# Keeping the running decay products in each chunk's buffer set instead of passing them through DRAM, with 20 sets in place of 23, in an RWKV-style attention and mixture-of-experts kernel

## The chip, the cores and the metric

The kernel runs on one core of a Trainium2 chip. The metric is the device time of one execution, in microseconds (us), lower being better. All arithmetic is in float32, or in float32 split into a rounded part and a remainder.

## The reference, cut to what matters

A linear recurrence over 768 tokens runs for 4 batches and 8 heads of width 40. Its outputs are then the tokens of a small mixture of 8 experts, with a gate that is balanced by eight rounds of row and column normalisation.

```python
for t in range(S):                                # 768 tokens; B=4, H=8, D=40
    y[:, :, t] = einsum('bhd,bhde->bhe', r_t, state)
    Sa = einsum('bhde,bhe->bhd', state, a_t)
    state_decay = state * w_t[:, :, None, :] - einsum('bhd,bhe->bhde', Sa, b_t)
    state = state_decay + einsum('bhd,bhe->bhde', v_t, k_t)
x = y as (3072 tokens, 320)
logits = x @ w_gate; logits = logits - logits.max()
P = exp(logits); 8 rounds: P /= rowsum + 1e-9; P /= colsum + 1e-9; P *= N / E
out = sum over 8 experts e of P[:, e] * (relu(x @ w1[e]) @ w2[e])   # w1 320x1024, w2 1024x320
```

## The kernel before, in words

The sequence is cut into 12 chunks of 64 tokens. A unit of work is one chunk of one batch, with all 8 heads as 4 pairs; there are 48 units, and unit number cb is chunk cb // 4, batch cb % 4. The two heads of a pair lie on partitions 0 to 39 and 64 to 103.

`prep` prepares one unit, and needs no state. It loads the decays w, k, b and a in one tile (`inp`, two buffers; the first units borrow memory of sets that aren't in use yet). VectorE (DVE) makes two running products of the decays with scans: `q` (L124, one buffer) and the decays `g` from the chunk's start (L134). GpSimd (POOL) multiplies k and b by q (`kb`, L147) and a by g (`ab`, L153 and L154); for the first six units VectorE does the two `ab`. TensorE then makes the products `ll` (L159) and transposes `kt` (L167). What the later steps need goes into one of NSX = 23 buffer sets, taken in turn: `sx`, `bb` and `cc`. The lower triangle `lt` is written to DRAM (`ld`). The decays g are written to DRAM too (L138, tile `gd`), to be read back (L278, tile `gl`) when the unit is computed.

Two chunks form a group. For each of the 6 groups 128 triangular 32x32 blocks are inverted on VectorE, one block per partition: `load_lu` reads them from `ld` into `lu` (L380), the functions of the list INV run, `finish` stores the inverses `un` and `tn` to DRAM (L371, L372). `tload` reads them back for one chunk, as `lb` (L243), `t1` and `t2` (tile `td`, L246 and L248) and the diagonal blocks of `tt` (L252), and `tmat` makes the off-diagonal part on TensorE (`gp`, `op`).

`recur` computes one unit in five steps, which alternate with those of other batches: load v, r and v transposed (`vz`, `rb`, `f`) and make `av` with VectorE's product into f (L290); `xc`; `pu`, with VectorE's product `pm`; `c2`, with VectorE's sum `ws` (L317), and on POOL the output `y`, which is ws times the decays (L321), and the next state `z` (L330, on VectorE from chunk 9); the transpose `zt`. r is used as a tile of 112 partitions by 128 columns for each pair, in which each head fills its own half of the columns and the rest is zero; two transfers of 48 KB write the filled parts, into two buffers that were zeroed at the start.

The order of the work is a list of (time, function) pairs, sorted and then traced. A unit's preparation stands in it behind the fourth step of the unit that had its set before, 23 units earlier, or later where the group's start P0 sets it. The traced program is put in order for each engine by a scheduler, and each engine runs its queue in that order. Almost all loads and stores are issued from the SyncE queue (SP), in one order as well.

In the second part (from L470 on), each expert's weights and the tokens are loaded, split into parts, and multiplied: `p` (L582) and `op` (L647). Its buffers use the memory of the attention's, so the first of its work starts as the attention's last units run. `sinkhorn` normalises the gate; `ident` and `ones`, which its transposes and sums need, and `pmat` are allocated before the attention.

Of the kernel before, what the change touches and what calls it, by code (L numbers as in the profile page):

```python
# [23 lines left out]
NTOK = NB * S  # L24
E, FF, DM = 8, 1024, 320
# [4 lines left out]
def attention(ctx, tc, d, xd, ps, pq, pt, gs, lg):  # L30
    nc = tc.nc
# [3 lines left out]
    const = ctx.enter_context(tc.tile_pool(name="a_const", bufs=1))  # L35
    io = ctx.enter_context(tc.tile_pool(name="a_io", bufs=1))
    wk = ctx.enter_context(tc.tile_pool(name="a_wk", bufs=2))
# [7 lines left out]
    ident = cst[:, 232:360]  # L45
    one65 = cst[0:RL, 400:660]

    NTB = 2
    sx_b, bb_b, cc_b = ([None] * NSX for _ in range(3))
    raws = {}  # L50
    for n in range(NCH * NB - NSX, NCH * NB):
        i, pool = n % NSX, sets[n - NCH * NB + NSX]
        if i in IN_SETS or i in KB_SETS:
            raw = pool.tile([128, 1252], F32, name=f"st{i}")
            raws[i] = raw
            sx_b[i] = raw[0:R2, 0:832].rearrange("r (p h x) -> r p h x", h=2, x=104)
# [30 lines left out]
    def clear():  # L87
        nc.gpsimd.memset(unf, 0.0)
        nc.gpsimd.memset(unf[:, 0:1024:33], 1.0)
        nc.gpsimd.memset(tnf, 0.0)  # L90
        for t in vz_b + rb_b + c1_b + lg_b:
            nc.vector.memset(t, 0.0)
        for t in y_b:
            nc.gpsimd.memset(t[96:RL], 0.0)
        for t in tt_b:
            nc.gpsimd.memset(t, 0.0)
# [18 lines left out]
    def prep(c, b, ld):  # L115
# [14 lines left out]
        i = next(j for j in range(NSX) if sx_b[j] is sx)  # L130
        bb, cc = bb_b[i], cc_b[i]
        ge = pin.tile([RL, NP, 65], F32, name="g", bufs=2)
        g = ge[:, :, 0:64]
        nc.vector.tensor_tensor_scan(  # L134
            out=ge.rearrange("r p t -> r (p t)"), data0=w65[:, 0:260],
            data1=g1.rearrange("r p t -> r (p t)"), initial=0.0, op0=ALU.mult, op1=ALU.add)
        gd = dr.tile([RL, 320], F32, name=f"gd{cb}", bufs=1)
        nc.sync.dma_start(out=gd[:, 0:260], in_=ge.rearrange("r p t -> r (p t)"))  # L138
        if cb < NKB:
# [37 lines left out]
        if cb >= NKB:  # L177
            (nc.sync if cb < N_SP else nc.scalar).dma_start(out=ld[GRP[c][1], :, b], in_=lt)
        return dict(cc=cc, g=gd, sx=sx, bb=bb)

# [52 lines left out]
    def tload(c):  # L233
        tt = rot("tt", tt_b)
        tts[c] = tt
        ld, ud, nd = invs[GRP[c][0]]
        t1, t2, lb = td_b[0][0:64], td_b[0][64:128], lg_b[0][0:64]
        cc = GRP[c][1]
        q = [slice(h * 32, h * 32 + 32) for h in range(2)]
        u = [[slice(cc * 64 + blk * 32 + h * 16, cc * 64 + blk * 32 + h * 16 + 16) for h in range(2)]  # L240
             for blk in range(2)]
        for h in range(2):
            nc.sync.dma_start(out=lb[q[h], :, q[h]],  # L243
                              in_=ld[cc, 0:32].rearrange("j b p h s -> j (b p) h s")[:, :, h, 32:64])
        for h in range(2):
            nc.sync.dma_start(out=t1[q[h]], in_=nd[u[0][h]].rearrange("g j s -> j g s"))  # L246
        for h in range(2):
            nc.sync.dma_start(out=t2[q[h]], in_=ud[u[1][h]].rearrange("g j s -> j g s"))  # L248
        for h in range(2):
            for blk in range(2):  # L250
                r = slice(h * 64 + blk * 32, h * 64 + blk * 32 + 32)
                nc.sync.dma_start(out=tt[r, :, r], in_=ud[u[blk][h]].rearrange("g j s -> j g s"))  # L252

# [16 lines left out]
    def recur(c, b):  # L270
# [3 lines left out]
        rb = rot("rb", rb_b)  # L274
        for h in range(2):
            nc.sync.dma_start(out=rb[h * 64:h * 64 + 48, :, h * 64:h * 64 + 64], in_=d["r"][c, b, h])
        gl = io.tile([RL, NP, 65], F32, name="gl", bufs=2)
        nc.sync.dma_start(out=gl.rearrange("r p t -> r (p t)"), in_=pp["g"][:, 0:260])  # L278
        f = wk.tile([R2, NP, 2, 104], F32, name="f", bufs=NFB)
# [40 lines left out]
        y = ys[c, b // 2]  # L320
        nc.gpsimd.tensor_tensor(out=y[0:R2, :, b % 2], in0=ws[:, :, 0:64], in1=gl[0:R2, :, 0:64], op=ALU.mult)  # L321
        if b % 2:
# [51 lines left out]
    def load_lu(s, n):  # L374
        ld = invs[s][0]
        for cc in range(n):
            for blk in range(2):
                for h in range(2):
                    u0, r0 = cc * 64 + blk * 32 + h * 16, blk * 32
                    nc.sync.dma_start(  # L380
                        out=lu[u0:u0 + 16],
                        in_=ld[cc, r0:r0 + 32].rearrange("j b p h s -> (b p) j h s")[:, :, h, r0:r0 + 32])

# [47 lines left out]
SKEW = 1.1  # L431
NSX = 23
GL = 3
# [32 lines left out]
def body(ctx, tc, d, out):  # L466
    nc = tc.nc
# [301 lines left out]
def _layout(inputs):  # L769
    g = {k: np.asarray(v, dtype=np.float32) for k, v in inputs.items()}  # L770

    def split(a):
        return a.reshape(NB, NP, 2, NCH, C, D).transpose(3, 0, 2, 5, 1, 4)

    def packed(a, fill=0.0):
# [60 lines left out]
```

## Time and profile before

| | |
|---|---|
| median of 3 runs | 1839.33 us (1838.09, 1839.33, 1847.54) |
| the profiled execution's own time | 1832.94 us |
| its span, first to last instruction | 1831.2 us, 31655 instructions |
| busy share of the span | PE 94%, DVE 75%, POOL 48%, ACT 47% |
| DMA packets | 211759, 140.47 MB; under 512 bytes 162965 |
| from DRAM and back, decays: `gd` and `gl` | 48 each, 113.8 KB each |
| loads of r | 96, 48.0 KB each |

"Busy" is the sum of an engine's instructions; a matrix product's end is modelled, so TensorE's 94% is not 94% of its peak. SPq is the queue of SyncE, whose only work is to issue transfers; PEclk is the granted clock of TensorE, 1.00 being full speed. The attention takes about the first 505 us, in which the DMA engines are busiest; the experts take the rest. In a row of a timeline the first two numbers are the start and the duration in us, and a bracket tells how long the engine had been idle and on what. In a row of a single line, the three numbers with strokes are the least, median and largest duration in ns.

### The profile page before, as it was taken

The page shows a single profiled execution, that of the slowest core. Times are in us where ns is not written, and L with a number is a line of the kernel's source. Part 1 is how long each engine was busy: PE and PEld are TensorE (multiplying, and loading weights), DVE is VectorE, ACT ScalarE, POOL GpSimd, SP SyncE. Part 2 cuts the span into 40 slices and gives each one's busy share as a digit, 9 for nine tenths or more (in the row PEclk, how much of TensorE's full clock was granted, in tenths as well). Part 3 has the DMA queues.
Part 4 walks back from the last instruction along what each step waited for, and adds up shares of the span by engine and source line. Part 5 has one row for each costly group of instructions (what it writes and reads, how often), then busy time and mean ns, then how long its engine had stood idle before and what let it go on. Part 6 is the DMA issues. An engine that isn't in the chain of part 4 may idle for free.

```text
span 1831.2 us, 31655 instructions
## 1 busy us (share of the span) xinstructions
PE 1724.3 (94%) x11843; PEld 1696.8 (93%) x11843; DVE 1365.3 (75%) x2356; ACT 856.8 (47%) x1851; POOL 874.0 (48%) x854
## 2 busy tenths in 40 slices
PE   4479988999989999999999999999999999999999
PEld 4368888898978999999999999999999999999999
DVE  7786996973788867777676878977686877767675
ACT  6347767766743533434343434345343343424342
POOL 6545664723462626447291735008182644628160
PEclk8568988999999999999999999999999999999999
DMA  7468777867520101111020112201020111102001
GB/s 193 116 157 185 175 180 174 186 137 172 152 77 20 57 20 57 38 39 57 20 75 20 57 37 61 69 1 60 16 76 20 57 38 38 57 20 75 15 24 44
DMA packets 211759, 140.47 MB, mean 77 GB/s; under 512 B 162965, under 2 KB 193813, under 8 KB 211605
## 3 DMA queue, kind: packets, MB, share of 16 engines
q1 hardware_dynamic: 207925, 132.70, 27.9%
q10 hardware_dynamic: 3680, 5.74, 1.2%
q8 instruction: 94, 1.54, 0.3%
q14 instruction: 60, 0.49, 0.1%
HBM read 110.78 MB, written 27.61 MB: 76 GB/s over the span
## 4 chain that ended last, share of the span: by engine, by line
PE 75%; DVE 7%; DMA 4%; issue 4%; POOL 3%; ACT 2%; SPq 2%; POOLq 0%; ACTq 0%; DVEq 0%
PE op L647 36%; PE p L582 33%; DMA inp<-in_inp_dram 1%; PE xc L297 1%; PE av L289 1%; PE pu L308 1%; DVE pr L193 1%; DVE hl L606 1%; DVE q L124 1%; PE c L315 1%; DMA ld<-lt 1%; PE op L266 1%; DVE sm L600 1%; PE ll L159 1%; POOL ab L154 1%
## 5 line engine op out<-in xcount | busy, mean ns | idle before, releaser
L582 PE MATMUL p<-xch,wh 128*128 128x384 f32 (+1 forms) x1792 | 605.0, 339 | 8.9 <-DVE sm L600 4.3
L603 ACT ACTIVATE hh<-sm 128x384 fp32r<-128x384 f32 x512 | 269.5, 527 | 728.5 <-DVE sm L600 728.4
L647 PE MATMUL op<-wh,hh 128*128 128x320 f32 x1536 | 477.2, 311 | 4.0 <-ACT hh L603 3.8
L647 PE MATMUL op<-wl,hh 128*128 128x320 f32 x1536 | 474.8, 310 | 0.0
L647 PE MATMUL op<-wh,hl 128*128 128x320 f32 x1536 | 468.0, 309 | 0.9 <-DVE hl L606 0.9
L528 POOL TENSOR_TENSOR wl<-ws,wh 128x640 fp32r<-128x640 f32 x60 | 103.1, 1718 | 606.2 <-ACT wh L526 606.1
L606 DVE SCALAR_TENSOR_TENSOR hl<-sm,hh 128x384 fp32r<-128x384 f32 x512 | 373.1, 762 | 2.6 <-ACT hh L603 1.8
L582 PEld LDWEIGHTS p<-xch,wh 128*128 128x128 f32 (+1 forms) x1792 | 337.0, 188 | 13.3 <-DVE sm L600 5.2
L582 PE MATMUL p<-xcl,wh 128*128 128x384 f32 x896 | 302.3, 337 | 0.0
L582 PE MATMUL p<-xch,wl 128*128 128x384 f32 x896 | 301.8, 337 | 0.0
L647 PEld LDWEIGHTS op<-wh,hh 128*128 128x128 f32 x1536 | 290.2, 189 | 4.9 <-ACT hh L603 4.9
L647 PEld LDWEIGHTS op<-wl,hh 128*128 128x128 f32 x1536 | 291.1, 190 | 0.0
L647 PEld LDWEIGHTS op<-wh,hl 128*128 128x128 f32 x1536 | 286.8, 188 | 1.4 <-DVE hl L606 1.2
L600 DVE TENSOR_TENSOR sm<-p,u 128x384 f32<-128x384 f32 x384 | 236.3, 625 | 8.7
L582 PEld LDWEIGHTS p<-xcl,wh 128*128 128x128 f32 x896 | 168.6, 188 | 0.0
L582 PEld LDWEIGHTS p<-xch,wl 128*128 128x128 f32 x896 | 168.5, 188 | 0.0
L600 DVE TENSOR_TENSOR sm<-p,p 128x384 f32<-128x384 f32 x128 | 71.3, 557 | 129.4 <-PE p L582 75.0
L600 DVE TENSOR_TENSOR p<-p,p 128x384 f32<-128x384 f32 x128 | 71.1, 556 | 101.7 <-PE p L582 101.4
L600 DVE TENSOR_TENSOR u<-p,p 128x384 f32<-128x384 f32 x128 | 70.8, 553 | 57.1 <-PE p L582 55.9
L536 POOL TENSOR_TENSOR wl<-ss,wh 128x512 fp32r<-128x512 f32 x60 | 90.3, 1505 | 28.4 <-ACT wh L533 24.2
L159 PE MATMUL ll<-ab,kb 104*128 104x128 f32 x336 | 62.8, 344 | 40.5 <-POOL kb L147 18.5
L159 PEld LDWEIGHTS ll<-ab,kb 104*128 104x128 f32 x336 | 54.2, 244 | 45.3 <-POOL kb L147 24.8
(163 smaller groups left out, 2727.3 us busy)
## 6 DMA issues: line engine op xcount, KB each, us to landing
ws<-in_wts_dram SPq DMA_DIRECT2D x60, 832.0 KB, 4.5
inp<-in_inp_dram SPq DMA_DIRECT2D x42, 451.5 KB, 4.5
gd<-g SPq DMA_DIRECT2D x48, 113.8 KB, 2.6
gl<-gd SPq DMA_DIRECT2D x48, 113.8 KB, 2.8
vz<-in_v_dram SPq DMA_DIRECT2D x48, 112.0 KB, 3.5
xd<-y SPq DMA_DIRECT2D x24, 224.0 KB, 3.5
ld<-lt ACTq DMA_DIRECT2D x40, 128.0 KB, 2.6
rb<-in_r_dram SPq DMA_DIRECT2D x96, 48.0 KB, 3.1
```

Source lines behind the costliest of these rows:

```text
L124: nc.vector.tensor_tensor_scan(out=qr.rearrange("r p t -> r (p t)"), data0=w65[:, 260:0:-1], data1=one65, initial=0.0, op0=ALU.mult, op1=A ...
L154: eng.tensor_tensor(out=ab[64:104, :, 64:128], in0=a_in[64:104], in1=g[64:104], op=ALU.mult)
L159: nc.tensor.matmul(ll[:, p], lhsT=kb[:, p], rhs=ab[:, p], start=True, stop=True)
L193: nc.vector.tensor_tensor(out=prv, in0=a.unsqueeze(2).broadcast_to([nu, n_c, n_r, n_k]), in1=m.unsqueeze(1).broadcast_to([nu, n_c, n_r, n_ ...
L266: nc.tensor.matmul(op[:, p], lhsT=gs[:, p], rhs=t2[:, p], start=True, stop=True)
L528: g.tensor_tensor(out=wl[:, 0:640], in0=raw[:, 256:896], in1=wh[:, 0:640], op=ALU.subtract)
L536: g.tensor_tensor(out=lv[:, 3:7], in0=so[:, :, 0], in1=hv[:, 3:7, 0], op=ALU.subtract)
L582: nc.tensor.matmul(o, lhsT=w_, rhs=x_, start=(j == 0), stop=(j == 3))
L600: eng.tensor_tensor(out=out, in0=x, in1=y, op=ALU.add)
L603: nc.scalar.activation(out=hh[:, f, h], in_=sm[f][:, h], func=AF.Relu)
L606: v.scalar_tensor_tensor(out=hl[:, f, h], in0=sm[f][:, h], scalar=0.0, in1=hh[:, f, h], op0=ALU.max, op1=ALU.subtract)
L647: nc.tensor.matmul(ops[i], lhsT=a[:, h, cs], rhs=w_[:, cw], start=(f == 0 and h == 0 and j == 0), stop=(last and h == 1 and j == 2))
```

## The change

The decays g are written straight into the unit's set (`ge`, 1040 bytes a partition), and `y` reads them there; the trip through DRAM and its two transfers a unit are gone. A set is therefore larger, and there are 20 instead of 23. r is laid out with its zeros in DRAM and comes in one transfer of 112 rows of 2048 bytes. The blocks of the inverse are ordered so that the two heads alternate, and `load_lu` and the two loads of `td` each take one transfer where two were needed. `pmat`, `ones` and `ident` are now allocated behind the attention, in memory that it used.

```diff
-        ge = pin.tile([RL, NP, 65], F32, name="g", bufs=2)
+        bb, cc, ge = bb_b[i], cc_b[i], ge_b[i]        # ge: a part of set i
         g = ge[:, :, 0:64]
         nc.vector.tensor_tensor_scan(out=ge..., data0=w65[:, 0:260], data1=g1..., ...)
-        gd = dr.tile([RL, 320], F32, name=f"gd{cb}", bufs=1)
-        nc.sync.dma_start(out=gd[:, 0:260], in_=ge.rearrange("r p t -> r (p t)"))
...
-        return dict(cc=cc, g=gd, sx=sx, bb=bb)
+        return dict(cc=cc, g=g, sx=sx, bb=bb)
... tload
-        for h in range(2):
-            nc.sync.dma_start(out=t1[q[h]], in_=nd[u[0][h]].rearrange("g j s -> j g s"))
-        for h in range(2):
-            nc.sync.dma_start(out=t2[q[h]], in_=ud[u[1][h]].rearrange("g j s -> j g s"))
+        nc.sync.dma_start(out=t1, in_=nn_[0])
+        nc.sync.dma_start(out=t2, in_=un_[1])
... recur
-        for h in range(2):
-            nc.sync.dma_start(out=rb[h * 64:h * 64 + 48, :, h * 64:h * 64 + 64], in_=d["r"][c, b, h])
-        gl = io.tile([RL, NP, 65], F32, name="gl", bufs=2)
-        nc.sync.dma_start(out=gl.rearrange("r p t -> r (p t)"), in_=pp["g"][:, 0:260])
+        nc.sync.dma_start(out=rb, in_=d["r"][c, b])
...
-        nc.gpsimd.tensor_tensor(out=y..., in0=ws[:, :, 0:64], in1=gl[0:R2, :, 0:64], op=ALU.mult)
+        nc.gpsimd.tensor_tensor(out=y..., in0=ws[:, :, 0:64], in1=pp["g"][0:R2], op=ALU.mult)
... load_lu
-                for h in range(2):
-                    nc.sync.dma_start(out=lu[u0:u0 + 16], in_=ld[cc, r0:r0 + 32]...[:, :, h, r0:r0 + 32])
+                nc.sync.dma_start(out=lu[u0:u0 + 32],
+                                  in_=ld[cc, r0:r0 + 32].rearrange("j b p h s -> (b p h) j s")[:, :, r0:r0 + 32])
...
-NSX = 23
+NSX = 20
... body, behind the attention and the experts' own buffers
+    two = ctx.enter_context(tc.tile_pool(name="two", bufs=1))
+    pmat, ones, ident = ...                            # from two
+    nc.gpsimd.memset(ones, 1.0)
+    nc.sync.dma_start(out=ident, in_=d["cst"][:, 232:360])
```

The program issues 533 transfers from SP where it issued 725: 48 fewer each of `gd`, `gl` and `rb`, 24 of `lu`, 12 each of the two `td`. The zeroing of `rb` is gone, and three units' sets less are cleared at the start.

The queue of SP at the end of the first group's inverse, before (names: `ud`, `nd` the stored inverses in DRAM, `ld` the triangles of the second group; the last two are the data of units 18 and 19):

```order
L371 DMA ud_244<-un_235 64x1024 x2
L372 DMA nd_245<-tn_239 64x1024 x2
L248 DMA td_219<-ud_244 32x16x32
L246 DMA td_219<-nd_245 32x16x32
L380 DMA lu_236<-ld_576 16x32x32 x4
L246 DMA td_219<-nd_245 32x16x32
L248 DMA td_219<-ud_244 32x16x32
L252 DMA tt0_217<-ud_244 32x16x32 x4
L138 DMA gd16_1002<-g_1000 112x260
L138 DMA gd17_1088<-g_1086 112x260
L118 DMA inp_1162<-in_inp_dram 112x1032
L118 DMA inp_1222<-in_inp_dram 112x1032
```

The same place of SP's queue now:

```order
L364 DMA ud_232<-un_223 64x1024 x2
L365 DMA nd_233<-tn_227 64x1024 x2
L244 DMA td_207<-ud_232 64x16x32
L372 DMA lu_224<-ld_534 32x32x32 x2
L243 DMA td_207<-nd_233 64x16x32
L248 DMA tt0_205<-ud_232 32x16x32 x4
L119 DMA inp_1072<-in_inp_dram 112x1032
L119 DMA inp_1129<-in_inp_dram 112x1032
```

Between the inverses' store and the next `inp` stand 8 transfers instead of 14; the load from `nd` now stands behind those of `lu`, where half of it stood ahead of them.

VectorE where unit 4 is computed and a later unit is prepared, before (g is the scan of unit 24, into a buffer of its own; ws that of unit 4):

```order
L134 SCALAR_TENSOR_TENSOR g_1566<-inp_1561,g10_223 112x260
L317 TENSOR_TENSOR ws_1657<-c2_1652,c10_229 104x416
L124 SCALAR_TENSOR_TENSOR q_1667<-inp_1665,cst_162 112x260
L310 TENSOR_TENSOR pm_1703<-pu_1698,cst_162 128x416
L128 RECIPROCAL g10_223<-q_1667 112x4
L134 SCALAR_TENSOR_TENSOR g_1670<-inp_1665,g10_223 112x260
```

VectorE at the same unit now (ge4 is the decay tile of set 4, which unit 4 leaves and unit 24 takes):

```order
L283 TENSOR_TENSOR f_1407<-av_1411,cst_147 104x8x64
L310 TENSOR_TENSOR ws_1528<-c2_1523,c10_217 104x416
L167 TENSOR_TENSOR sx3_185<-ll_1453,cst_147 64x8x64
L134 SCALAR_TENSOR_TENSOR ge4_192<-inp_1536,g10_211 112x260
L303 TENSOR_TENSOR pm_1571<-pu_1566,cst_147 128x416
L125 SCALAR_TENSOR_TENSOR q_1620<-inp_1618,cst_147 112x260
```

The scan of unit 24 stood ahead of `ws` of unit 4; now it stands one instruction behind it. It overwrites what `y` of unit 4 reads, and so waits for POOL. This is so for units 20 to 47, each against the unit 20 before it.

POOL at that place now (kb and ab on ge4 are unit 24's, cc5 is unit 25's):

```order
L150 COPY cc4_191<-q_1538 104x4
L314 TENSOR_TENSOR y0_221<-ws_1528,ge4_192 104x4x64
L323 TENSOR_TENSOR z_1531<-ws_1528,cc8_151 104x160
L145 TENSOR_TENSOR kb_1542<-inp_1536,q_1538 104x512
L151 TENSOR_TENSOR ab0_209<-inp_1536,ge4_192 40x4x64
L152 TENSOR_TENSOR ab0_209<-inp_1536,ge4_192 40x4x64
```

Before, `kb` and both `ab` of unit 24 stood ahead of `y` of unit 4; now they stand behind it.

More of the change, by code (lines that the diff above doesn't have):

```diff
@@ L35, in attention @@
     const = ctx.enter_context(tc.tile_pool(name="a_const", bufs=1))
-    io = ctx.enter_context(tc.tile_pool(name="a_io", bufs=1))
     wk = ctx.enter_context(tc.tile_pool(name="a_wk", bufs=2))
@@ L48, in attention @@
     NTB = 2
-    sx_b, bb_b, cc_b = ([None] * NSX for _ in range(3))
+    sx_b, bb_b, cc_b, ge_b = ([None] * NSX for _ in range(4))
     raws = {}
@@ L53, in attention @@
         if i in IN_SETS or i in KB_SETS:
-            raw = pool.tile([128, 1252], F32, name=f"st{i}")
+            raw = pool.tile([128, 1512], F32, name=f"st{i}")
             raws[i] = raw
@@ L58, in attention @@
             cc_b[i] = raw[0:R2, 1248:1252]
+            ge_b[i] = raw[0:RL, 1252:1512].rearrange("r (p t) -> r p t", t=65)
             continue
@@ L62, in attention @@
         cc_b[i] = pool.tile([R2, NP], F32, name=f"cc{i}")
+        ge_b[i] = pool.tile([RL, NP, 65], F32, name=f"ge{i}")
     tt_b = [const.tile([128, 4 * NP, 128], F32, name=f"tt{i}") for i in range(NTB)]
@@ L90, in clear @@
         nc.gpsimd.memset(tnf, 0.0)
-        for t in vz_b + rb_b + c1_b + lg_b:
+        for t in vz_b + c1_b + lg_b:
             nc.vector.memset(t, 0.0)
@@ L130, in prep @@
         i = next(j for j in range(NSX) if sx_b[j] is sx)
-        bb, cc = bb_b[i], cc_b[i]
-        ge = pin.tile([RL, NP, 65], F32, name="g", bufs=2)
+        bb, cc, ge = bb_b[i], cc_b[i], ge_b[i]
         g = ge[:, :, 0:64]
@@ L239, in tload @@
         q = [slice(h * 32, h * 32 + 32) for h in range(2)]
-        u = [[slice(cc * 64 + blk * 32 + h * 16, cc * 64 + blk * 32 + h * 16 + 16) for h in range(2)]
-             for blk in range(2)]
+        un_, nn_ = ([t[cc * 64 + blk * 32:cc * 64 + blk * 32 + 32].rearrange("(g h) j s -> (h j) g s", h=2)
+                     for blk in range(2)] for t in (ud, nd))
         for h in range(2):
@@ L251, in tload @@
                 r = slice(h * 64 + blk * 32, h * 64 + blk * 32 + 32)
-                nc.sync.dma_start(out=tt[r, :, r], in_=ud[u[blk][h]].rearrange("g j s -> j g s"))
+                nc.sync.dma_start(out=tt[r, :, r], in_=un_[blk][h * 32:h * 32 + 32])
     def tmat(c, half):
@@ L320, in recur @@
         y = ys[c, b // 2]
-        nc.gpsimd.tensor_tensor(out=y[0:R2, :, b % 2], in0=ws[:, :, 0:64], in1=gl[0:R2, :, 0:64], op=ALU.mult)
+        nc.gpsimd.tensor_tensor(out=y[0:R2, :, b % 2], in0=ws[:, :, 0:64], in1=pp["g"][0:R2], op=ALU.mult)
         if b % 2:
@@ L377, in load_lu @@
             for blk in range(2):
-                for h in range(2):
[L379 to L382, printed above, removed]
+                u0, r0 = cc * 64 + blk * 32, blk * 32
+                nc.sync.dma_start(out=lu[u0:u0 + 32],
+                                  in_=ld[cc, r0:r0 + 32].rearrange("j b p h s -> (b p h) j s")[:, :, r0:r0 + 32])
     ev = [(T_CLEAR, clear, ())]
@@ L472, in body @@
     one = ctx.enter_context(tc.tile_pool(name="one", bufs=1))
-    pmat = one.tile([128, 24, E], F32, name="pmat")
     lg = one.tile([128, 24, E], F32, name="lg")
-    ones = one.tile([128, 128], F32, name="ones")
-    ident = one.tile([128, 128], F32, name="ident")
     gs = one.tile([R2, NP, E], F32, name="gs")
@@ L483, in body @@
         attention(actx, tc, d, xd, ps, pq, pt, gs, lg)
-        nc.gpsimd.memset(ones, 1.0)
-        nc.sync.dma_start(out=ident, in_=d["cst"][:, 232:360])
     stg = ctx.enter_context(tc.tile_pool(name="stg", bufs=2))
@@ L490, in body @@
     x1 = ctx.enter_context(tc.tile_pool(name="x1", bufs=1))
+    two = ctx.enter_context(tc.tile_pool(name="two", bufs=1))
+    pmat = two.tile([128, 24, E], F32, name="pmat")
+    ones = two.tile([128, 128], F32, name="ones")
+    ident = two.tile([128, 128], F32, name="ident")
+    nc.gpsimd.memset(ones, 1.0)
+    nc.sync.dma_start(out=ident, in_=d["cst"][:, 232:360])
     po = ctx.enter_context(tc.tile_pool(name="po", bufs=1, space=bass.MemoryType.PSUM))
@@ L787, in _layout @@
                           np.zeros((NCH, NB, RL, 56), np.float32)], -1)
-    rb = np.zeros((NCH, NB, 2, 48, NP, C), np.float32)
-    rb[:, :, :, 0:40] = split(g["r"])
+    rb = np.zeros((NCH, NB, RL, NP, 2 * C), np.float32)
+    x = split(g["r"])
+    rb[:, :, 0:40, :, 0:C], rb[:, :, 64:104, :, C:] = x[:, :, 0], x[:, :, 1]
     vt = g["v"].reshape(NB, NH, NCH, C, D).transpose(2, 0, 3, 1, 4).reshape(NCH, NB, C, NH * D)
```

## The prediction

> **What bounds the kernel now.** I read the busy times by stage first, then what VectorE waits for in the stage that waits most, then the SP queue's own rows. The windows cut the run at the first `pm` (124 us), at about the last preparation (360), at the attention's end (505) and where the hand-over to the experts is done (560).
>
> ```profile
> core 0: us, PE busy (x) PEld busy (x) DVE busy (x) ACT busy (x) POOL busy (x), PEclk, DMA share, GB/s
> 0.00:124.00 124.00, 64.89 (x344) 58.20 (x344) 93.71 (x169) 57.85 (x144) 72.65 (x104) 0.63 0.64 155
> 124.00:360.00 236.00, 211.34 (x1956) 202.58 (x1957) 195.04 (x333) 168.38 (x424) 141.35 (x164) 0.91 0.79 179
> 360.00:505.00 145.00, 139.42 (x1361) 133.39 (x1360) 87.66 (x161) 96.81 (x232) 49.57 (x62) 0.96 0.66 153
> 560.00:1831.00 1271.00, 1262.79 (x7927) 1259.97 (x7925) 943.63 (x1622) 510.82 (x1007) 580.77 (x500) 1.00 0.13 42
> ```
>
> The last stage is TensorE's (1262.79 of 1271 us at full clock, DMA engines at 0.13). The change touches nothing in it, so all that can move lies in the first 505 us. In 0 to 124 no engine is full: a chain through preparations, stores, the first inverse and loads sets the length. In 124 to 360 VectorE is busy for 195 of 236 us and TensorE for 211, at 0.91 of its clock; each waits for the other and for transfers. In 360 to 505 TensorE is nearly full (139 of 145). So a change that removes transfers can only gain where a transfer or SP's queue ends a wait. Those of VectorE in the middle stage:
>
> ```profile
> DVE q L124 <- DMA inp<-in_inp_dram: 16.6, 8, 5.6
> DVE q L124 <- POOL kb L147: 3.1, 4, 1.8
> ```
>
> Of 41 us (236 less 195) the late load of `inp` takes 16.6, the largest single item.
>
> **The transfers removed.** What one costs SP's queue (least, median, largest ns of one issue):
>
> ```profile
> L138 SPq DMA_DIRECT2D gd<-g x48: 303/320/1346, 15.2 to 367.3; - x48
> L278 SPq DMA_DIRECT2D gl<-gd x48: 303/431/1358, 20.9 to 494.6; - x48
> L276 SPq DMA_DIRECT2D rb<-in_r_dram x96: 564/594/1667, 5.8 to 481.0; - x96
> L380 SPq DMA_DIRECT2D lu<-ld x48: 303/484/1532, 40.3 to 376.4; - x48
> L246 SPq DMA_DIRECT2D td<-nd x24: 420/600/1057, 104.6 to 464.6; - x24
> L248 SPq DMA_DIRECT2D td<-ud x24: 317/478/1875, 102.8 to 466.1; - x24
> ```
>
> By medians: 48 x (0.320 + 0.431 + 0.594) + 24 x 0.484 + 12 x (0.600 + 0.478) = 64.6 + 11.6 + 12.9 = 89 us of SP's time. That isn't 89 us of the run, since SP isn't on the path most of the time. The bytes:
>
> ```profile
> gd<-g SPq DMA_DIRECT2D x48, 113.8 KB, 2.6
> gl<-gd SPq DMA_DIRECT2D x48, 113.8 KB, 2.8
> rb<-in_r_dram SPq DMA_DIRECT2D x96, 48.0 KB, 3.1
> ```
>
> `gd` and `gl` free 96 x 113.8 KB = 10.9 MB. r grows from 96 x 48 KB = 4.6 MB to 48 x 224 KB (112 rows of 2048 bytes) = 10.8 MB. So 4.7 MB fewer in all, and 112 pieces of 2048 bytes in place of 2 x 48 x 4 of 256. I cost the larger r at nothing: it is loaded one to two units ahead, and VectorE's product behind `av` hides it. If that cover went, one landing (3.1 us) could show.
>
> Now by stage, each with its price.
>
> **Start, 0 to 124 us.** Two places where SP is late.
>
> ```profile
> 39.91 0.30 SPq L138 DMA_DIRECT2D gd<-g  x1
> 40.31 1.49 SPq L380 DMA_DIRECT2D lu<-ld  x3
> 41.84 1.65 SPq L162 DMA_DIRECT2D ld<-st  x1
> ...
> 45.41 0.45 POOL L102 MEMSET st<- 128x416 f32 x1 [2.39 <-DMA ld<-st]
> 45.93 1.18 POOL L147 TENSOR_TENSOR kb<-st,q 104x512 f32<-104x512 f32 x1
> ...
> 59.83 0.27 DVE L200 COPY lu<-lu 128x128 f32<-128x128 f32 x1 [1.19 <-DMA ld<-lt]
> ```
>
> POOL waits 2.39 us at 45.41 for unit 5's store of `lt`, which sits in SP behind loads of `lu`, which sit behind a `gd` that waits for VectorE's scan. Without `gd`, and with two `lu` instead of three ahead of the store, it leaves about 2 us sooner, and unit 7's `kb` with it; that unit is the last that the first inverse (59.83) needs. I take 2 us (ends 0 and 2.39, the whole wait).
>
> ```profile
> 105.49 1.89 SPq L380 DMA_DIRECT2D lu<-ld  x4
> 110.95 0.95 SPq L138 DMA_DIRECT2D gd<-g  x2
> 112.00 0.89 SPq L118 DMA_DIRECT2D inp<-in_inp_dram  x2
> ...
> 110.03 0.27 DVE L200 COPY lu<-lu 128x128 f32<-128x128 f32 x1 [4.48 <-DMA td<-nd]
> 117.02 0.70 DVE L124 TENSOR_TENSOR_SCAN q<-inp,cst 112x260 f32<-112x260 f32 x1 [0.91 <-DMA inp<-in_inp_dram]
> ```
>
> At the end of the first inverse two `lu` (half of 1.89), a `td` (0.6) and two `gd` (0.95) fall away ahead of the `inp` at 112.00, some 2.5 us. VectorE waited 0.91 for it at 117.02, and 4.48 at 110.03 for `lu`, whose last issue comes 0.9 earlier. I take 2 us of those 5.4. Start: -4 us, ends -8 (2.4 + 5.4) and 0.
>
> **Middle, 124 to 360 us.** One of the eight waits of `inp`, in full:
>
> ```profile
> 149.75 0.68 POOL L154 TENSOR_TENSOR ab<-inp,g 40x256 f32<-40x256 f32 x1
> ...
> 153.78 1.29 SPq L278 DMA_DIRECT2D gl<-gd  x1
> ...
> 156.45 0.46 SPq L118 DMA_DIRECT2D inp<-in_inp_dram  x1
> ...
> 162.46 0.70 DVE L124 TENSOR_TENSOR_SCAN q<-inp,cst 112x260 f32<-112x260 f32 x1 [5.08 <-DMA inp<-in_inp_dram]
> ```
>
> The buffer came free at 150.43, when the last reader (L154) ended; the load left SP at 156.45, six us late, behind r, four stores of the inverse, `gl`, `xd` and `gd`. Without `gl` (1.29), the `gd` and one r, some 2.5 us of the six go: half of the wait of 5.08. Half of the 16.6 is a gain of 8 (ends 0, if other rows of the queue take the place, and 16.6).
>
> Against it stands the new wait. The scan of unit n + 20 (n from 0 to 27: 28 scans) now waits for POOL's `y` of unit n, which waits for `ws`, one to six rows ahead of that scan in VectorE's own queue. Behind the waiting scan stand `pm`, the next `q` and the next f, for which TensorE waits.
>
> ```profile
> L321 POOL TENSOR_TENSOR y<-ws,gl x48: 677/687/1657, 130.3 to 504.4; 104x256 f32<-104x256 f32 x48
> L147 POOL TENSOR_TENSOR kb<-inp,q x40: 1175/1180/2213, 50.4 to 360.6; 104x512 f32<-104x512 f32 x40
> ```
>
> `y` takes 0.69, at most 1.66; the row between `ws` and the scan (`sx` or `pm`) covers about 0.55, an estimate somewhat under the 0.70 of the scan q at 117.02. So a scan waits between 0.1 and 1.1 us: 28 x 0.1 = 3 and 28 x 1.1 = 31. I take 3, nearest the median of `y`. Middle: -8 + 3 = -5, ends -17 and +31. That three units fewer are prepared ahead moves work between the stages and adds none: 20 units were prepared before the first `pm`, and still are. In VectorE's queue the last group's inverse ends behind `pm` of unit 36 where it ended behind `ws` of unit 34, with four units left before unit 40 needs it; I cost that at nothing, and one unit (145 us over 22 units, 6.6 us) if that cover were gone.
>
> **Tail and hand-over, 360 to 560 us.** TensorE loses time here where a load of the experts' weights, late in SP, holds ScalarE's queue:
>
> ```profile
> 438.35 1.63 PE L297 MATMUL xc<-f,st 104*104 104x104 f32 x16
> 442.82 1.06 PE L308 MATMUL pu<-x,tt 128*128 128x104 f32 x8
> 448.35 1.12 PE L289 MATMUL av<-rb,vz 104*104 104x128 f32 x8 [1.78 <-ACT vz L338]
> ...
> 454.75 2.03 PE L308 MATMUL pu<-x,tt 128*128 128x104 f32 x8
> 456.58 2.98 PE L297 MATMUL xc<-f,sx 104*104 104x104 f32 x16
> ```
>
> After the wait of 1.78 the same products take 2.03 for 1.06 and 2.98 for 1.63, so about half the clock; from 449.5 to 459.6, ten us, that loses 4 to 5 by estimate, and 6 with the wait. `gl` and one r a unit less make that load earlier. Whether the stall goes is luck of place; I take half, -3, ends -6 and +6 (a like one elsewhere).
>
> `ident` moves behind the last stores of the attention; the transpose that reads it:
>
> ```profile
> 495.01 10.89 SPq L324 DMA_DIRECT2D xd<-y  x2
> 512.18 0.27 PE L667 MATMUL mp<-ident,mxs 128*1 128x128 f32 x1
> ```
>
> Issued at 506 and landing within the 2 to 4.5 us of the rows above, it is there by 510.5, ahead of 512.18: nothing; 3 us if it slips behind other work. `ones`, a clear on POOL, is short beside its idle time there.
>
> **Sum.** -4 - 5 - 3 = -12 us, on the profiled execution's 1832.94 us (span 1831.2): 1821. The median of the three runs shown is 6.4 us higher, 1839.3, so the forecast for the median is 1827.
>
> **What a page would make of it.** A rule speaks against the gain: the Trainium skill, DMA: Bandwidth & Descriptors, section Issuing engines are not separate DMA queues, says that the sequencer's time to start a transfer "is usually small relative to the DMA itself". By that rule the 89 us are worth nearly nothing, and the middle stage keeps its 16.6; the sum would then be the second rival's, below. The trace half agrees: an issue of r is 0.594 against 3.1 to land, but the queue stood six us behind at 156.45.
>
> **The rivals.** First, slower: the scans in lock step. If `kb` and `z` also come ahead of what the next `q` needs (on POOL now `y`, `z`, `kb` in a row, 0.69 + 0.43 + 1.18 = 2.3 us behind `ws`, `z` estimated from `y` by its 160 elements a row to 256), VectorE waits about 1 us a unit, 28 us in all, while the gains stay -12 + 3 = -15: +13 or, with the gain of `inp` lost since its load starts later, about +20. Time 1855. For it: VectorE is busy in 195 of 236 us already, so a wait in most units has little room. Against: the wait for `kb` was only 3.1 us in this stage. It decides from about 0.9 us a scan on, where 28 x 0.9 = 25 outweighs the 15 and the 9.2 of the bound below.
>
> Second, nothing much changes: SP isn't what is late, other rows fill the same waits, and only the start's 4 us come: 1835. For it: TensorE at 211 of 236. Against: the load at 156.45.
>
> Third, more: with the waits of `inp` (16.6) gone and TensorE's clock in the middle risen from 0.91 by some 0.03 (7 of 211 us), -4 - 16 - 7 = -27: 1812.
>
> **How the numbers follow.** Three runs spread by 9 us; 0.5% (9.2 us) is about the least that a measurement of this kernel tells from no change. Forecast 0.45 (1818 to 1837; two thirds of it beyond -9.2), lock step 0.20, nothing 0.22, more 0.13. Faster: 0.30 + 0.13 + 0.02 = 0.45. Slower: 0.17 of the lock step and 0.02 of the rest, 0.19. The same: 0.36. The range runs from 1808, below the third rival, to 1852, just short of the lock step's centre, which leaves under 2 in 10 outside.
>
> **What would show it.** Right: the first `pm` at about 120 us; waits of `q` for `inp` of 8 us or less between there and the last preparation; waits of the scan `g` on `y` of 3 us in sum; DMA share below 0.79 in the middle. Wrong: waits of VectorE on POOL's `y` or `kb` of 15 us or more; TensorE's clock under 0.91 in the middle; a first `pm` at 124; the transpose with `ident` later than ten us after the attention's end.

## The result, and the profile after

The changed kernel took 1822.99 us (median of 4 runs, 1819.04 to 1826.42) beside 1840.9 for the kernel before on the same chip: ratio 0.9897, 95% interval 0.9858 to 0.9935. On a second chip, with more runs of the kernel before, it was 1822.57 beside 1834.12: 0.9938 (0.9926 to 0.9950). The intervals overlap; by the medians the gain is 17.9 us in the first comparison and 11.5 in the second. The two profiled executions of the first lie closer, 1832.94 and 1826.19 us, because that of before was quicker than the four other runs beside it.

The changed kernel by the cuts of the prediction (the same columns):

```profile
0.00:124.00 124.00, 65.42 (x356) 59.00 (x356) 96.79 (x171) 59.69 (x149) 72.73 (x102) 0.63 0.62 148
124.00:360.00 236.00, 221.46 (x2117) 212.49 (x2118) 198.53 (x342) 177.32 (x447) 140.20 (x168) 0.94 0.78 175
360.00:505.00 145.00, 137.55 (x1238) 130.51 (x1236) 87.15 (x153) 89.08 (x210) 48.09 (x58) 0.92 0.59 133
560.00:1824.00 1264.00, 1256.35 (x7878) 1253.57 (x7876) 931.43 (x1610) 507.30 (x999) 574.97 (x496) 1.00 0.13 42
```

The middle does more (2117 products of TensorE in the same 236 us against 1956) at a higher clock, 0.94 against 0.91. The third stage does fewer, 1238 against 1361, at 0.92 against 0.96. The experts are untouched. What VectorE waits for in 124 to 360 us in the changed kernel:

```profile
DVE q L125 <- DMA inp<-in_inp_dram: 15.4, 6, 4.6
DVE q L125 <- POOL kb L145: 1.1, 2, 0.6
DVE ge L134 <- POOL y L314: 0.2, 1, 0.2
```

The wait that the forecast was to halve, 16.6 us, is 15.4 (19.8 in a second execution). The feared wait of the scan for `y` came once and cost 0.2.

Fixed cuts mix stages that begin at other times, so from here on each run is cut at its own marks: `ws` of unit 0, of unit 27 and of unit 47 on VectorE. "Start" is what lies ahead of the first, "middle" runs to unit 27, "tail" to unit 47. Middle and tail of before, of the changed kernel, and of the changed kernel's second execution:

```profile
129.55:372.98 243.43, 220.90 (x2067) 211.91 (x2066) 195.66 (x337) 175.98 (x445) 143.75 (x167) 0.92 0.79 179
372.98:503.72 130.74, 125.73 (x1219) 120.30 (x1218) 80.40 (x148) 84.60 (x202) 45.24 (x55) 0.96 0.65 151
```

```profile
128.26:354.51 226.25, 212.59 (x2049) 203.94 (x2048) 191.15 (x331) 170.34 (x431) 136.62 (x163) 0.95 0.78 174
354.51:496.11 141.60, 135.02 (x1238) 128.06 (x1236) 86.07 (x152) 88.83 (x212) 47.96 (x58) 0.92 0.63 143
```

```profile
128.38:357.10 228.72, 210.69 (x2048) 201.84 (x2047) 189.80 (x332) 170.08 (x431) 140.01 (x163) 0.95 0.79 172
357.10:492.64 135.54, 130.03 (x1237) 123.52 (x1236) 85.35 (x151) 88.81 (x212) 47.72 (x58) 0.95 0.66 150
```

These rows are an account that closes. A stage's length less TensorE's busy time is its idle time, and the length times one less the granted clock is what the clock took. Middle before: 22.5 us idle and 0.08 x 243 = 19 of clock; after: 13.7 and 0.05 x 226 = 11. Without both, 202 and 201 us are left. So the change took no work off TensorE: it gained 9 us of idle time and 8 of clock. The tail went the other way: idle 5.0 to 6.6, clock 0.04 x 131 = 5 to 0.08 x 142 = 11. Some of the shift is work that moved: in the changed kernel VectorE does 4.5 us less in the middle and 5.7 more in the tail (with 20 sets alone 2.8 less and 1.1 more). Middle and tail together: 374.2 us before, 367.9 and 364.3 after. From `ws` of unit 47 to the end both kernels take the same, 1327.5 and 1328.2 us.

### The profile page after: what moved, and what is told of

Its sections match the earlier page's. It is cut to its first block, busy times and chain, and to the rows that moved or that the text cites. A ratio compares the mean times of both kernels' runs of the same rounds, so it can differ in the third digit from the quotient of the medians.

```text
span 1824.3 us, 31326 instructions
## 1 busy us (share of the span) xinstructions
PE 1727.8 (95%) x11843; PEld 1700.0 (93%) x11843; DVE 1363.8 (75%) x2354; ACT 856.0 (47%) x1848; POOL 868.5 (48%) x851
## 4 chain that ended last, share of the span: by engine, by line
PE 79%; DVE 9%; DMA 4%; issue 3%; POOL 2%; ACT 2%; SPq 1%; ACTq 0%; POOLq 0%; DVEq 0%
PE op L639 36%; PE p L574 33%; PE xc L290 2%; PE av L282 1%; DVE pr L191 1%; PE pu L301 1%; PE c L308 1%; PE ll L157 1%; PE gp L257 1%; DVE q L125 1%; DMA lu<-ld 1%; DVE sm L592 1%; DMA rb<-in_r_dram 1%; POOL kb L145 1%; PE op L262 1%
## 6 DMA issues: line engine op xcount, KB each, us to landing
ld<-lt ACTq DMA_DIRECT2D x40, 128.0 KB, 3.0
```

## The experiments

All times are ratios to the kernel before on the same chip; stages are in us, of one profiled execution each.

| kernel | ratio (95%) | start | middle | tail | middle + tail |
|---|---|---|---|---|---|
| before | 1 | 129.6 | 243.4 | 130.7 | 374.2 |
| changed | 0.9897 (0.9858 to 0.9935) | 128.3 | 226.3 | 141.6 | 367.9 |
| changed, again | 0.9938 (0.9926 to 0.9950) | 128.4 | 228.7 | 135.5 | 364.3 |
| 20 sets alone | 0.9954 (0.9935 to 0.9974) | 126.4 | 240.8 | 130.3 | 371.0 |
| clears in another sequence | 0.9963 (0.9943 to 0.9983) | 123.4 | 242.3 | 130.0 | 372.4 |
| a clear done twice | 1.0022 (1.0000 to 1.0043) | 126.5 | 245.7 | 135.8 | 381.5 |
| decays on chip, 20 sets | 0.9925 (0.9905 to 0.9945) | 128.3 | 234.3 | 133.9 | 368.2 |
| r in one transfer | 0.9881 (0.9858 to 0.9905) | 123.8 | 234.1 | 130.2 | 364.3 |
| heads alternate | 0.9924 (0.9903 to 0.9944) | 128.8 | 239.3 | 128.4 | 367.7 |
| r and heads | 0.9943 (0.9929 to 0.9956) | 125.3 | 236.5 | 129.2 | 365.7 |
| changed, weights cast on POOL | 0.9962 (0.9940 to 0.9985) | 127.5 | 222.5 | 140.3 | 362.8 |
| changed, weights and x cast on POOL | 0.9943 (0.9921 to 0.9964) | 127.7 | 229.9 | 136.5 | 366.4 |
| changed, 4 buffers for f, 19 sets | 0.9982 (0.9966 to 0.9999) | 128.0 | 235.8 | 137.5 | 373.3 |
| changed, 240 empty transfers | 1.0110 (1.0079 to 1.0142) | 123.3 | 254.0 | 143.5 | 397.4 |

### The parts one by one

Theory A: the gain is SP's time for the transfers removed. Theory B: it is the order that 20 sets give. Theory C, first named with r: any edit makes the scheduler draw another order, and the draw is what counts.

**20 sets alone.**

```
-NSX = 23
+NSX = 20
```

> The kernel before with 20 sets in place of 23, nothing else. Theory A (the time came from transfers and SP's issue time): no gain, 1841 to 1846 us, and ws of unit 27 stays at about 373 us. Theory B (the time came from the order: with 20 sets the preparation of unit n+20 stands one to one beside unit n): the middle stage gains most of the change's 17 us, ws of unit 27 at 357 to 362, time 1825 to 1832.

Ratio 0.9954, ws of unit 27 at 367.1. Both theories miss. A expected no gain, and there is one of 0.5%. B's range of times holds (1827.95 us, beside 1836.79 for the kernel before on this chip), but the gain is in the start (-3.2) and the middle (-2.7), not the 17 us in the middle that B expected. As the whole cause B falls.

**The decays on the chip alone** (with the 20 sets that they need, and with `pmat`, `ones` and `ident` behind the attention as in the changed kernel).

```
-        gd = dr.tile([RL, 320], F32, name=f"gd{cb}", bufs=1)
-        nc.sync.dma_start(out=gd[:, 0:260], in_=ge.rearrange("r p t -> r (p t)"))
...
-        nc.sync.dma_start(out=gl.rearrange("r p t -> r (p t)"), in_=pp["g"][:, 0:260])
...
-        nc.gpsimd.tensor_tensor(out=y[0:R2, :, b % 2], in0=ws[:, :, 0:64], in1=gl[0:R2, :, 0:64], op=ALU.mult)
+        nc.gpsimd.tensor_tensor(out=y[0:R2, :, b % 2], in0=ws[:, :, 0:64], in1=pp["g"][0:R2], op=ALU.mult)
```

> The changed kernel with r in two transfers again and the heads of the block inverse in one after the other (as before): only the decays stay on the chip, with 20 sets. Theory A: SP saves 36 of the 89 us (48 x 0.320 + 48 x 0.431), so about 0.4 of the gain: 1834. Theory B: nearly the whole gain, 1823 to 1828, ws of unit 27 at 355 to 360.

0.9925, 1822.14 us: more than A's share. The time is about that of B (1823 to 1828), but `ws` of unit 27, at 362.6, comes later than B's 355 to 360.

**r in one transfer alone.**

```
-        for t in vz_b + rb_b + c1_b + lg_b:
+        for t in vz_b + c1_b + lg_b:
...
-        for h in range(2):
-            nc.sync.dma_start(out=rb[h * 64:h * 64 + 48, :, h * 64:h * 64 + 64], in_=d["r"][c, b, h])
+        nc.sync.dma_start(out=rb, in_=d["r"][c, b])
...
```

> The kernel before with r in one transfer that carries its zero halves, nothing else (23 sets, decays through memory). Theory A: SP saves 48 x 0.594 = 28.5 us, about 0.3 of the gain: 1835. Theory B: within 5 us of before, 1836 to 1846. Theory C (each build draws another order of instructions and another pattern of stalls, worth plus or minus 8 us whatever is removed): anywhere from 1833 to 1849, with the difference in the tail behind unit 27.

0.9881, 1815.51 us: as much as the whole change, and quicker than all three theories expected. Start and middle of this kernel:

```profile
0.00:123.84 123.84, 66.25 (x362) 59.72 (x363) 96.05 (x174) 61.05 (x152) 73.09 (x105) 0.64 0.69 166
123.84:357.91 234.07, 218.76 (x2079) 208.61 (x2078) 192.59 (x337) 176.24 (x446) 138.87 (x167) 0.94 0.88 204
```

The DMA engines are busier than before (0.88 for 0.79, 204 GB/s for 179) and the middle is 9 us shorter. So bytes are not what the middle waits for; here fewer transfers came with a gain although they carry more. Of the 15.6 us by which its tail ends earlier, 5.7 were there at the first `ws`. This kernel also drops rb's clears at the start, and a build below that only moves those clears has as much there.

**The alternating heads alone.**

```
-                for h in range(2):
-                    u0, r0 = cc * 64 + blk * 32 + h * 16, blk * 32
-                    nc.sync.dma_start(
-                        out=lu[u0:u0 + 16],
-                        in_=ld[cc, r0:r0 + 32].rearrange("j b p h s -> (b p) j h s")[:, :, h, r0:r0 + 32])
+                u0, r0 = cc * 64 + blk * 32, blk * 32
+                nc.sync.dma_start(out=lu[u0:u0 + 32],
+                                  in_=ld[cc, r0:r0 + 32].rearrange("j b p h s -> (b p h) j s")[:, :, r0:r0 + 32])
...
-        for h in range(2):
-            nc.sync.dma_start(out=t1[q[h]], in_=nd[u[0][h]].rearrange("g j s -> j g s"))
+        nc.sync.dma_start(out=t1, in_=nn_[0])
...
```

> The kernel before with the heads alternating in the block inverse (4 lu fewer a group of two chunks and 2 td fewer a chunk), nothing else. Theory A: SP saves 11.6 + 12.9 = 24.5 us, 0.27 of the gain: 1836, with the second group's inverse 1 to 3 us earlier (110.0 before). Theory B: within 5 us of before. Theory C: 1833 to 1849.

0.9924, 1823.32 us, quicker than all three theories expected; the gain is in the middle (-4.1) and the tail (-2.3). By middle and tail together the three parts gain 6.0, 9.9 and 6.4 us, the whole change 6.3 and 9.9. They do not add up, and r with the heads, run later, shows it again.

> The kernel before with r in one transfer and with the alternating heads, 23 sets and the decays through memory. If the parts add up (r alone gave 0.9881, the heads alone 0.9924): 0.980 to 0.982, about 1802. If each part only shortens the same waits, or the order that is drawn decides half of it: 0.985 to 0.992, 1810 to 1823. ws of unit 27 at 350 to 354 in the first case, at 356 to 368 in the second.

0.9943, 1823.87 us: less gain than r alone, and a little less than the second case expected; middle and tail 365.7 against 364.3 of r alone.

### What a draw of the order is worth

Two edits to the kernel before remove nothing and make the scheduler draw another order: rb's clear goes to the end of its list of clears; or one clear is done twice.

```
-        for t in vz_b + rb_b + c1_b + lg_b:
+        for t in vz_b + c1_b + lg_b + rb_b:
```

> The kernel before with one list of clears at the start in another sequence (rb's last), nothing removed: the same instructions, but the scheduler puts some 250 of VectorE's 2358 rows in other places, as many as r in one transfer moves (235). Theory C (the order drawn is what the parts were worth): anywhere from 1815 to 1845, a difference of 4 us or more from before, about as likely quicker as slower. Theory A (the transfers removed are what they were worth): 1837 within 3 us, ws of unit 27 at 370 to 376.

```
+    nc.vector.memset(g1_b[0], 0.0)
```

> The kernel before with one clear of 112x260 on VectorE done twice at the start (some 0.3 us, ahead of the first load's landing): 146 of VectorE's rows move. Theory C: 4 us or more from before, either way. Theory A: 1837 within 3 us, ws of unit 27 at 370 to 376.

The first is quicker (0.9963), the second slower or the same (1.0022). The first is as theory C expected, 6.5 us from the kernel before by the medians; the second, 4.0 us from it, is at C's least and within A's 1837 plus or minus 3 (1837.74, ws of unit 27 at 372.2). So a draw was worth 0.4% one way and 0.2% the other, up to half of what the parts gave. Where it shows matters. Start and middle of the first:

```profile
0.00:123.36 123.36, 66.08 (x358) 60.27 (x358) 96.95 (x176) 61.18 (x152) 73.85 (x105) 0.62 0.67 163
123.36:365.68 242.32, 224.72 (x2080) 215.50 (x2079) 197.08 (x338) 175.78 (x445) 142.70 (x167) 0.91 0.79 182
```

Its gain is in the start (-6.2); the middle is that of before. Over the four builds with the transfers of before the middle is 240.8 to 245.7 and middle and tail 371.0 to 381.5. Over the eight executions with fewer transfers they are 222.5 to 239.3 and 362.8 to 368.2; not counted are the empty transfers, and f's four buffers, which have 235.8 and 373.3. The groups do not touch, though by one execution of each build and by 1.5 us in the middle and 2.8 in the sum, where the builds that remove nothing spread by 4.9 and 10.5 among themselves. So the start goes with the draw, and the middle's gain goes with the removed transfers in all eight; that they cause it is likely, not proved.

### SP's time alone

```
+    def idle(cb, js):
+        for j in js:
+            nc.sync.dma_start(out=dm[cb, j:j + 1], in_=cst[0:1, 0:16])
...
+        idle(cb, (0, 1))
...
+        idle(c * NB + b, (2, 3, 4))
```

> The changed kernel with 5 transfers of 64 bytes a unit added to SP's queue (2 in the preparation, 3 in the recurrence; constant to memory, nobody waits for them): 240 issues of 0.3 to 0.4 us, some 80 us of SP's time, without bytes. Theory A (SP's issue time is what was worth the gain): ws of unit 27 back to 368 to 375 us, 1835 to 1842. Theory C: within the draws, 1815 to 1832, with waits of q for inp no longer than 20 us in the middle.

1.0110, 1856.3 us: past theory A's range. The added transfers, and the middle:

```profile
L52 SPq DMA_DIRECT2D dm<-cst x240: 214/251/1424, 4.8 to 487.3; - x120
```

```profile
123.27:377.25 253.98, 234.56 (x2068) 223.50 (x2068) 193.87 (x332) 171.83 (x434) 135.86 (x163) 0.87 0.65 155
```

240 x 0.251 = 60 us of SP's time, nearly no bytes (DMA share down to 0.65), and middle and tail are 30 to 33 us longer than in the changed kernel; no draw came near that. It isn't a clean proof of A: the order is redrawn here too (some 330 of VectorE's 2357 rows), up to unit 15 nothing is lost (ws at 252.6 against 255.8), most of the loss is clock (0.13 x 254 = 33 us, against 11 in the changed kernel), and the transfers cost more than their issue: between 124 and 360 us SP stood 7.2 us at them for stores of `lt` and 2.3 for loads of `inp`. Theory C's range is missed as well.

### The tail

In the changed kernel's tail the rows of ScalarE, TensorE and SP read:

```profile
431.34 0.83 ACT L514 CAST wh<-ws 128x768 fp32r<-128x768 f32 x1 [5.32 <-DMA f<-in_vt_dram]
```

```profile
430.50 0.98 PE L338 MATMUL lp<-gs,y 104*128 104x8 f32 x8
434.56 0.98 PE L308 MATMUL c<-pm,bb 128*104 128x104 f32 x8 [3.08 <-ACT c L297]
...
436.21 2.03 PE L301 MATMUL pu<-x,tt 128*128 128x104 f32 x8
```

```profile
423.84 0.63 SPq L502 DMA_DIRECT2D ws<-in_wts_dram  x1
...
431.23 4.85 SPq L248 DMA_DIRECT2D tt<-ud  x4
```

A cast of the experts' weights holds ScalarE's queue for 5.32 us. (The row names f; the cast reads `ws`.) Its load left SP at 423.84, some two us ahead of the cast's turn, and landed 7.3 us later; the median of such loads is 4.4. TensorE then waits 3.08, and the next `pu` takes 2.03 for 1.06. It is the stall that the prediction read in the tail of before, at another place and longer. First try: the 8 casts of the first two weight tiles go to POOL, which is busy for 48 of the tail's 142 us.

```
-        nc.scalar.copy(out=wh[:, 640:1408], in_=raw[:, 896:1664])
+        cast = g.tensor_copy if k < 2 else nc.scalar.copy
+        cast(out=wh[:, 640:1408], in_=raw[:, 896:1664])
```

> The changed kernel with the casts of the experts' first two weight tiles (8 instructions) on POOL in place of ScalarE. Theory: in the tail ScalarE's queue is held 5.3 us by the cast that waits for the late weights, and TensorE then runs at half clock for some ten us, which is the 11 us that the tail gave back; without it ws of unit 27 to ws of unit 47 takes 128 to 134 us in place of 141.6, time 1810 to 1815. Rival (the tail's loss is made elsewhere, by the order of the loads or by prepared x): 138 us or more, 1819 to 1825.

The tail stayed at 140.3, and the time, 1827.80 us, is above both expectations. The next cast in ScalarE's queue, that of x, took the place:

```profile
437.29 0.83 ACT L549 CAST xch<-xs 128x768 fp32r<-128x768 f32 x1 [6.16 <-DMA xs<-xd]
```

```profile
426.36 4.56 SPq L248 DMA_DIRECT2D tt<-ud  x4
```

```profile
SPq L248 <- DMA ws<-in_wts_dram: 2.7, 2, 1.4
```

The last two of its five loads stand in SP behind a `tt`, and `tt`, by SP's row of waits, stands for the loads of the weights, still in flight. TensorE waits 3.45 us at 438.93 for a copy behind that cast, and its clock is at half from 438 to 462 us, the longest such stretch of any tail. So the casts of x went to POOL as well, beside a plain repeat of the changed kernel on the same chip.

```
-        nc.scalar.copy(out=xh[:, 0:3, :, cu], in_=bv)
+        cast = nc.gpsimd.tensor_copy if s == 0 else nc.scalar.copy
+        cast(out=xh[:, 0:3, :, cu], in_=bv)
```

> The changed kernel with all casts for the first two weight tiles and for the first three pieces of the experts' x (17 instructions) on POOL in place of ScalarE. In the run with the weights' casts alone on POOL the tail stayed at 140.3: ScalarE was held 6.16 us by the next cast in its queue, that of x, whose loads stand in SP behind a tt that waits 4.6 us. Theory (late loads reach TensorE through ScalarE's casts): the stall of 3 us and over at 430 to 440 us is gone, the tail takes 128 to 135 us, and the time is 0.984 of before, 7 to 12 us under the changed kernel's. Rival (the tail's loss is the tt and r loads themselves, whoever casts): tail 138 us or more, 0.990.

> The changed kernel once more, unchanged, on the chip of the next two. Theory (the tail's loss lies in the order: loads late in SP hold ScalarE in every execution): 0.990 of before, ws of unit 27 to ws of unit 47 again 138 to 144 us, with TensorE's idle time there over 6 us. Rival (it was a bad moment of the one execution, since a stretch at half clock begins where a stall happens to meet the clock's own rhythm): the tail of this profile differs by 5 us or more from 141.6, with the same instructions in the same order.

The repeat: tail 135.5, 6.1 us from the first, and TensorE's idle time 5.5. By these numbers the rival holds. But the stall, which the theory is about, came again in the same place, and half clock after it:

```profile
436.45 1.72 PE L308 MATMUL c<-pm,bb 128*104 128x104 f32 x8 [2.80 <-ACT c L297]
...
439.09 2.03 PE L301 MATMUL pu<-x,tt 128*128 128x104 f32 x8
```

What was absent is the first execution's second stretch at half clock, from 459 to 474 us (about 7 us lost). So the stall lies in the order, and some 6 of the 11 us that the tail gave back were that one execution's. With the casts of x on POOL too the tail is 136.5 and the ratio 0.9943, a miss of the theory's 128 to 135 and 0.984: TensorE's idle time rose from 5.5 to 12.2 us. The late x now holds VectorE's queue instead, and TensorE waits for the `ws` behind it, until 449.08. The longer wait, for a `z`, ends at 469.72; VectorE has rows that split x ahead of that `z`, but waits for no load there. VectorE's and TensorE's waits in that tail:

```profile
DVE xt L547 <- DMA xs<-xd: 5.7, 1, 5.7
```

```profile
PE zt L328 <- DVE z L323: 5.5, 1, 5.5
PE av L282 <- DVE ws L310: 3.4, 1, 3.4
```

In these executions the late load reached TensorE through whichever queue touched it first. Neither version beats the changed kernel.

### What SP stands behind

Between 124 and 360 us SP stands still for a buffer of f in the changed kernel; in the kernel before, hardly. There it was two of the removed transfers that held SP: `gl`, whose buffer `y` had still to read, and `gd`, which waited for the scan. The rows of SP's waits, after and before:

```profile
SPq L273 <- PE xc L290: 22.6, 9, 4.1
```

```profile
SPq L278 <- POOL y L321: 12.5, 9, 2.7
SPq L138 <- DVE g L134: 10.6, 12, 1.7
...
SPq L280 <- PE xc L297: 0.8, 1, 0.8
```

So 23.1 us of standing went with the decays' trip through DRAM, which the prediction priced by its issues alone, and 22.6 came in at f (22.6 also with the decays on the chip alone, 1.9 with 20 sets alone).

```
-NFB = 3
+NFB = 4
-NSX = 20
+NSX = 19
```

> The changed kernel with four buffers for f in place of three, and 19 sets in place of 20 to make room. Theory (in the changed kernel SP stands still behind loads of f that wait for a buffer, 22.6 us in the middle, and the loads of inp behind them come as late as before): the wait of SP for f's buffer falls under 8 us, q waits for inp 8 us or less between 124 and 360 us (15.4 to 16.6 before), ws of unit 0 to ws of unit 27 takes 216 to 222 us in place of 226 to 229, 0.988 to 0.990 of before. Rival (inp has two buffers, and its load can't start before the preparation two units ahead has read its own; SP's standing still only fills that time): q still waits 12 us or more for inp, SP now waits for POOL's ab and cc at inp's load instead, 0.992 to 0.996.

Inconclusive. SP still waits 20.7 us for f's buffer, so the edit did not remove what it was to remove; q waits 21.3 us for `inp`, and the time is 0.9982. Whether f's loads are what keeps `inp` late stays open.

## Why the prediction was right, and where

The time, the sign and the sum (-12 us; measured -17.9 and, in the narrower measurement, -11.5) came out. The terms did not: -4, -5 and -3 were forecast for start, middle and tail, and the two profiled executions of the changed kernel show -1.3, -17.2, +10.9 and -1.2, -14.7, +4.8. That they add up to about the forecast is luck.

- **Start, -4: wrong.** The inverses do begin earlier: 59.83 became 55.15 and 110.03 became 104.43, so 4.7 and 5.6 us where 2 and 4 were taken. But that the removed transfers did it is not shown. The kernel before with the clears in another sequence, which removes nothing, has both at nearly the same times:

```profile
54.79 0.27 DVE L200 COPY lu<-lu 128x128 f32<-128x128 f32 x1 [1.05 <-DMA ld<-lt]
...
104.73 0.27 DVE L200 COPY lu<-lu 128x128 f32<-128x128 f32 x1 [4.25 <-DMA td<-nd]
```

  With 240 empty transfers added they stand at 53.35 and 104.14. Nor did the lead last: the first `pm` starts at 124.25 (124.02 before), which the prediction had named as a sign of being wrong, and the first `ws` is only 1.3 us earlier. VectorE after, then before:

```profile
104.43 0.27 DVE L198 COPY lu<-lu 128x128 f32<-128x128 f32 x1 [3.79 <-DMA lu<-ld]
...
110.35 0.70 DVE L125 TENSOR_TENSOR_SCAN q<-inp,cst 112x260 f32<-112x260 f32 x1 [2.09 <-DMA inp<-in_inp_dram]
...
122.23 0.67 DVE L194 TENSOR_REDUCE un<-pr 128x64 f32<-128x512 f32 x1
122.93 0.27 DVE L205 COPY tn<-un 128x128 f32<-128x128 f32 x1
123.11 1.22 DVE L191 TENSOR_TENSOR pr<-un,lu 128x1024 f32<-128x1024 f32 x1
124.25 0.58 DVE L303 TENSOR_TENSOR pm<-pu,cst 128x416 f32<-128x416 f32 x1
```

```profile
124.02 0.58 DVE L310 TENSOR_TENSOR pm<-pu,cst 128x416 f32<-128x416 f32 x1
124.52 0.67 DVE L196 TENSOR_REDUCE un<-pr 128x64 f32<-128x512 f32 x1
125.22 0.30 DVE L207 COPY tn<-un 128x128 f32<-128x128 f32 x1
125.44 1.21 DVE L193 TENSOR_TENSOR pr<-un,lu 128x1024 f32<-128x1024 f32 x1
```

  At the `un` of 122.23 (124.52 before) 2.3 of the 5.6 us are left; 1.2 of those lost are a longer wait for `inp`, 2.09 for 0.91. Then the three pieces of the second inverse that stood behind `pm` stand ahead of it. The step that failed took the first `pm` to follow the inverse at a fixed distance; the order puts it elsewhere in VectorE's queue. The redrawn clears, which remove nothing, had the first `ws` 6 us earlier.
- **Middle, -8 for the waits of `inp`: wrong mechanism.** They stayed (16.6 to 15.4 and 19.8), and across all runs their sum does not go with the middle's length: 13.0 us in the slowest draw of before (middle 245.7), 10.5 with the heads alternating (239.3), 19.8 in the repeat (228.7). The gain was larger than forecast, 15 to 17 us, of which a part only moved to the tail (VectorE's work there grew by 5 to 6 us), and lies in TensorE's idle time (-9 and -4) and its clock (-8). The forecast's sum had nothing for the clock; the third rival had 7 us for its rise by 0.03, which came, but tied it to the waits of `inp`, which stayed. Which of TensorE's waits carries it was not settled: no single row accounts for it.
- **+3 for the scans behind `y`: too much.** It is the lower end of the prediction's own 3 to 31, 0.1 us for each of 28 scans; one scan waited, 0.2 us. The lock step, given 0.20, did not come.
- **Tail, -3 with ends of 6: too narrow.** +11 in the first execution, +5 in the second: work moved there, the stall of 1.78 us came back as 3.08 and 2.80, and the half clock after it lasted as long (10 us) or longer (14).
- **Costs of nothing.** The larger r and the later `ident` were hidden: the transpose that reads `ident` runs at 504.5 us with no wait ahead of it. (The prediction's "2 to 4.5 us of the rows above" misreads them, since the landings shown there are 2.6 to 3.1; nothing hung on it.) Three sets fewer did not cost: alone they gave 0.9954.
- **The 89 us of SP's time.** 60 us of empty issues made the kernel 1.1% slower than before, and each part that removes 24 to 36 us of issue was 0.8 to 1.2% quicker, where builds that remove none came out at -0.5% to +0.2%. The Trainium skill, DMA: Bandwidth & Descriptors, section Issuing engines are not separate DMA queues, calls the time to start a transfer usually small beside the transfer. For one transfer that holds here (0.594 us against 3.1 for r); the second rival, built on it, is not what these runs show. But the parts do not add up. SP's standing still in the middle, all rows of that view added up, rises from 66 to 115 us, which would fit an SP that has become early; that this is the reason is argued, not shown.

## What to carry to other kernels

Where a scheduler sets the order, time a few edits that remove nothing before believing a part's gain: here they moved the kernel by 0.4% one way and 0.2% the other, gave the inverses the very lead that the prediction had put down to the change, and only cutting each run at its own marks set the draw (start) apart from what went with the change (middle). Make the account close first: length = work + TensorE's idle time + clock, and price a short wait at its length plus the half clock that may follow it. Price a transfer not by its issue alone but also by what the queue stands for at it. When a late load holds an engine's queue, moving the reader to another engine can move the stall with it, as it did twice here; issuing the load earlier was not tried.

## What the runs showed of the hardware

TensorE's clock fell to half after short waits, and stayed there while TensorE was busy. In the kernel with the empty transfers:

```profile
256.41 0.54 PE L336 MATMUL zt<-cst,z 104*40 104x104 f32 x4 [1.21 <-POOL z L331]
...
258.14 2.04 PE L309 MATMUL pu<-x,tt 128*128 128x104 f32 x8 [0.24 <-ACT c L305]
...
264.39 3.10 PE L298 MATMUL xc<-f,sx 104*104 104x104 f32 x16
...
277.74 2.98 PE L298 MATMUL xc<-f,sx 104*104 104x104 f32 x16
...
290.31 1.63 PE L298 MATMUL xc<-f,sx 104*104 104x104 f32 x16
```

A wait of 1.21 us, then 31 us in which `xc` takes 3.10 and 2.98 for 1.63 with no wait over 0.24 between. In the clock records of the 14 profiled executions there are 108 stretches at half clock that begin between 118 and 500 us. Each is a multiple of 3.41 us long: 41 of one, 33 of two, 24 of three, 8 of four, one of seven (weights cast on POOL) and this one of nine. By 95 of them a wait of 0.7 us or more stands within 3.5 us of the beginning. The other way round it is a matter of length: of the waits that began at full clock, 41 of 102 between 0.7 and 1.5 us had a drop within 3.5 us of their end, 29 of 39 between 1.5 and 2 us, and 32 of 33 from 2 us on. The Trainium skill, TensorE: Matmul & The Clock Gate, section Why this matters for your kernels, warns of idle gaps over about 3 us between bursts. The traces have the drop after shorter ones too, and the same wait in the same order was followed by 10 us at half clock in one execution and 14 in the other.
